# Moving one sum and its gate activation in the first and the last of eight output pairs

## The chip, the cores and the metric

The kernel runs on one core of a Trainium2 chip. The metric is the device time of one execution in microseconds (us). Times of before: a median of 366.15 us over three runs, from 365.76 to 366.25.

The engines are named as the profile names them: PE is TensorE (matmuls; PEld its weight loads), DVE is VectorE, ACT is ScalarE, POOL is GpSimd, SP is the engine that issues most of the transfers (DMA).

## The reference, cut to what matters

```python
x = A_x                                    # (1, 2048, 512)
xn = layernorm(x)
s = irfft2(rfft2(xn) * (w_r + 1j * w_i))   # spectral branch, the "way back" ends it
h = layernorm(xn)
u = gelu(einsum("bsd,sf->bdf", h, w1) + b1)        # token MLP, hidden size 1792
y = einsum("bdf,fs->bds", u, w2) + b2
out = x + s * silu(y.transpose(0, 2, 1))           # the gate is silu(y)
```

## The kernel before

All matmuls are fp32 in effect: each operand is split into a high part (a rounded copy, made by ACT) and a low part (the rest, a subtraction on DVE), and three matmuls are accumulated: high by high, high by low, low by high.

The first 200 us or so compute the layer norms, the first transform, the hidden layer (`u`) and the filter of the spectral branch. The last 160 us are the output stage, and the change lies there.

**Pairs.** The output has 16 row blocks of 128 tokens. They are handled as 8 pairs p = 0 to 7: block p (gate tile `g0`) and block p+8 (gate tile `g1`), each of 512 channels in two halves (`left_`, `right_`). A pair's product with the second weight matrix is a 2 by 2 block product, done in Strassen's manner with seven products instead of eight. A product (`products(p, n)`) is 21 matmuls of 256 columns. Its number n names the form of `u` that it reads: 1 is `fd`, 2 and 3 are `fa`, 5 and 6 are `fc`, 4 and 7 are `fb` in the profile. The products run in the order `ORDER = (1, 2, 5, 6, 3, 7, 4)`, into three PSUM areas: `bx` (one of two banks, by pair), `by`, `bz`.

**Sums of a pair.** Copies of partial products (`p1`, `p5`, `v2`, on ACT) and sums on DVE (all named `c` in the profile) give the four results:

- after product 2: `c11 = by + p1`, the left half of `g0` (its gate activation is issued after product 6);
- after product 3: `c12 = bz + v2`, the right half of `g0`. This is the sum that the change moves. In the profile it is `c<-ps,v`;
- after product 7: `c22 = bx + p5`, the right half of `g1` (`c<-ps,p`, as `c11` is);
- product 4 goes on accumulating in `bx`, the bank that `c22` reads, so its first matmul waits for `c22`. The left half of `g1` is gated straight from that bank.

A gate activation is one Silu on ACT, `g<-c,b2t` in the profile.

**Weights of the products.** `w2_forms()` is a generator of weight tiles `w2f`, each made by one ACT copy of 128x896 (high part) and one DVE subtraction (low part), from tiles `a12`, `a11`, `a21` (profile: `a`) and `s1`, `s4` (profile: `s`), which are loaded by SP and, for the sums of blocks, added to by POOL. There are three `w2f` buffers. The loop takes the next weights by `next(wforms)` after each product, about three products ahead: after product 3 of pair 0 come the weights of product 1 of pair 1, called `1_1` here, made from the `a12` tile that is loaded for pair 1.

**The way back of the spectral branch.** For each pair: `yt` copies (ACT and DVE), small matmuls (`even_channels`, `odd_channels`: `ps<-cd,yt`), then sums on DVE (`unfolded`: the tiles `es`, then two operations that write `y`), then eight matmuls (`spectral`: `ps<-y,cft`), and then `finish`, which multiplies by the gate and writes the block out. `SLOTS` lists by hand behind which product each piece stands. In pairs 0 to 6 the spectral matmuls and the multiplications run one pair late. In the last pair they follow at once: the `es` sums stand behind product 6, the two `y` operations behind product 3, the spectral matmuls behind product 7 and in front of product 4.

**Order.** In this stage every engine's instructions keep the program's order (`Kept`), so a position in the loop is a position in the queue of DVE, ACT, PE and SP.

In the loop, `k` counts the positions in `ORDER`; product 3 is `k == 4`. `more` is false in the last pair only.

Of the kernel before, what the change touches and what calls it, by code (L numbers as in the profile page):

```python
# [141 lines left out]
def spectral_mixer_kernel(tc, x, w1, b1, w2, b2, wk, we, wx, c_f, c_ft, c_d, c_i, c_g, c_h, out):  # L142
# [7 lines left out]
    def mirrored(t, turned):  # L150
        v = t.rearrange("p (h q c) -> p h q c", q=2, c=P)
        return v[:, :, 0], v[:, :, 1, ::-1] if turned else v[:, :, 1]
# [9 lines left out]
    with tc.tile_pool(name="ps", bufs=1, space=PSUM) as psp, ExitStack() as left, ExitStack() as right:  # L162
# [345 lines left out]
        for j in range(NJ):  # L508
            more = j + 1 < NJ
# [275 lines left out]
        for n in range(8):  # L785
            a, b, c, d, e, f = PACE[n]
# [51 lines left out]
        def sums_of_blocks():  # L838
            added_up("a12", "s1")
            added_up("a11", "a12")  # L840
# [58 lines left out]
        left_, right_, whole = slice(0, HD), slice(HD, D), slice(0, D)  # L899
        quarter_rows = slice(0, P), slice(P, HD)  # L900

        def banks(p):
            return ps[:, 2 + p % 2, :HD], ps[:, 4, :HD], ps[:, 5, :HD]

        def products(p, n):

            wf = ready.pop(0)
            bx, by, bz = banks(p)
            o = {1: bx, 6: bx, 7: bx, 4: bx, 2: by, 5: bz, 3: bz}[n]

            for a, (wi, ui) in enumerate(((0, 0), (0, 1), (1, 0))):
                for m, i in enumerate(FORMS):
                    T.matmul(o, wf[:, wi, i], form_parts(n, i)[ui], start=m + a == 0 and n in (1, 2, 5),
                             stop=m == NH - 1 and a == 2, skip_group_check=n in (6, 3, 7, 4))

        def copied(name, src, where):
            t = where.tile([P, HD], F32, name=name, tag=name.split("_")[0], bufs=1)
            step(A.activation(t, src, AF.Copy))
            return t
# [25 lines left out]
        def new_gates(p):  # L945
            return [fp.tile([P, D], F32, name=f"g{j}", tag="g", bufs=4) for j in (p, p + NP)]
# [6 lines left out]
        def gathered(p):  # L953


            yt = fp.tile([P, 2, 4, 2, 64], F32, name=f"yt{p}", tag="yt")
            yts[p] = yt
            for i, j in enumerate((p, p + NP)):
                for h in range(2):
                    to = yt[:, i, :, h ^ i].rearrange("p b (s c) -> p b s c", c=2)  # L960
                    yield V.tensor_copy(to, ey[:, :, h::2, j]) if i else A.activation(to, ey[:, :, h::2, j], AF.Copy)
# [4 lines left out]
        def even_channels(p):  # L966


            for i in range(2):
                for s in range(2):  # L970
                    at = slice(128 * i + 64 * s, 128 * i + 64 * s + 64)
                    for e in range(2):
                        for r, rows in enumerate((slice(0, 64), slice(64, P))):
                            T.matmul(ps[64 * e:64 * e + 64, 6 + r, at], yts[p][rows, i, 2 * s, e], ci[rows, 2 * s, :64],
                                     start=True, stop=True)
# [8 lines left out]
        def unfolded(p):  # L984

            es, y = new_sums(p) if p else first_sums
            e0, e1 = (es[:, :, k].rearrange("p i b c -> p i (b c)") for k in range(2))
            first, odd = ps[:, 6, :256].rearrange("p (i s c) -> p i s c", s=2, c=64), ps[:, 6:8, 256:]
            other = y.rearrange("p i h q c -> p (i h q c)")[:, :257]
            A.activation(other, ps[:, 7, :257], AF.Copy)  # L990
            other = other[:, :256].rearrange("p (i s c) -> p i s c", s=2, c=64)

            V.tensor_add(es[:, :, 1, :, :64], first, other)
            V.tensor_sub(es[:, :, 1, 0, :63:-1], first[:, :, 0], other[:, :, 0])
            V.tensor_sub(es[:, :, 1, 1, :63:-1], other[:, :, 1], first[:, :, 1])
            V.tensor_add(e0, e1, odd)
            V.tensor_sub(e1, e1, odd)
            yield
            u, v = es[:, :, :, 0], es[:, :, :, 1]
            V.tensor_add(y[:, :, :, 0], u, v)  # L1000
            yield
            V.tensor_sub(y[:, :, ::-1, 1], u, v)
            ys[p] = y.rearrange("p i h q c -> p i (h q c)")
            yield
# [9 lines left out]
        def gate(g, j, cols, src, scale):  # L1014
            A.activation(g[:, cols], src, AF.Silu, bias=b2t[:, j:j + 1], scale=scale)

        def summed(name, a, b):
            t = fp.tile([P, HD], F32, name=name, tag="c", bufs=2)
            V.tensor_add(t, a, b)
            return t  # L1020

        def finish(g, j, cols):
            r = last_rows[:, j // NP] if last_rows is not None else fp.tile([P, D], F32, name=f"r{j}", tag="r", bufs=2)
            for to, a, b in zip(mirrored(r[:, cols], True), mirrored(ps[:, j // NP, cols], False), mirrored(g[:, cols], False)):
                V.tensor_mul(to, a, b)
            if last_rows is not None:
                for part in quarter_rows if cols is left_ else (cols,):
                    V.tensor_add(r[:, part], r[:, part], xr[j // NP][:, part])
            for queue, (rows, tokens) in zip((SY, SY if cols is right_ else A), halved):
                if last_rows is None:  # L1030
                    G.dma_start(out[tokens, j, cols], r[rows, cols], accum_op=ALU.add)
                else:
                    queue.dma_start(out[tokens, j, cols], r[rows, cols])
# [4 lines left out]
        for p in range(NP):  # L1038
            j0, j1 = p, p + NP
            more = p + 1 < NP  # L1040
            if p:
                gates[p] = new_gates(p)
            g0, g1 = gates[p]
            bx, by, bz = banks(p)
            slot, plan = SLOTS[min(p, 2) + (not more)]
            gathering = gathered(p)
            for k, n in enumerate(ORDER):
                started = not p and k < 2
                if not started:
                    products(p, n)  # L1050
                if n == 1 and p:
                    p1 = copied(f"p1_{p}", bx, w2p)
                elif n == 5:
                    p5 = copied(f"p5_{p}", bz, fp)
                elif n == 6:
                    v2 = copied(f"v2_{p}", bx, fp)
                elif n == 7:
                    c22 = summed(f"c22_{p}", bx, p5)
                if not started:
                    ready.extend(w for w in [next(wforms, None)] if w is not None)  # L1060
                if n == 2:
                    c11 = summed(f"c11_{p}", by, p1)
                elif n == 6:
                    gate(g0, j0, left_, c11, 1.0)
                elif n == 3:
                    gate(g0, j0, right_, summed(f"c12_{p}", bz, v2), 1.0)
                elif n == 7:
                    gate(g1, j1, right_, c22, -1.0)
                elif n == 4:
                    for cols in (left_,) if more else quarter_rows:  # L1070
                        gate(g1, j1, cols, bx[:, cols], -1.0)
                if not p and k == slot - 1:
                    even_channels(p)
                if k == slot:
                    for part in PARTS[p]:
                        {"S": spectral, "E": even_channels, "O": odd_channels}[part](p - (part == "S"))
                    yts.pop(p)
                    pieces = unfolded(p)
                    if p:
                        for g, j in zip(gates.pop(p - 1), (j0 - 1, j1 - 1)):  # L1080
                            finish(g, j, whole)
                for what in plan.get(k, ""):
                    next(gathering if what == "g" else pieces)
                if more and n == 7:
                    sums_of_blocks()
                if not more and k == 2:
                    xr = [where.tile([P, NH * P], F32, name=f"xr{i}", tag="s1", bufs=1)[:, :D] for i, where in enumerate((w2p, fp))]
                    for to, j in zip(xr, (j0, j1)):
                        for rows, tokens in halved:
                            SY.dma_start(to[rows], x[tokens, j])  # L1090
                if not more and k == 5:
                    spectral(p)
                    last_rows = fp.tile([P, 2, D], F32, name="rows", tag="yt")
                    finish(g0, j0, whole)
                    finish(g1, j1, right_)
# [38 lines left out]
```

## Time and profile before

| | |
|---|---|
| median of 3 runs | 366.15 us (365.76 to 366.25) |
| the profiled execution, its own time | 366.07 us |
| its span in the trace | 364.3 us |
| PE busy | 357.4 us, 98% |
| DVE busy | 306.4 us, 84% |
| ACT busy | 211.1 us, 58% |
| POOL busy | 87.2 us, 24% |
| the chain that ended last, by engine | PE 90%, DVE 3%, DMA 3%, ACT 2%, issue 1% |

The span is the stretch that the trace covers; the execution's own time is 1.77 us longer. The chain that ended last is followed back from the last instruction, at each step to what released it. The rows stand in a section below.

### The profile page before, as it was taken

What the parts mean: (1) busy time and instruction counts of PE and PEld (TensorE: products, weight loads), DVE (VectorE), ACT (ScalarE), POOL (GpSimd) and SP (SyncE); (2) the same over time, 40 slices, a digit from 0 to 9 for tenths busy, and PEclk for the clock granted to TensorE, in tenths of its full rate; (3) what the DMA queues carried; (4) which work ended last, traced back from release to release, by engine and by line L of the source; (5) the groups of instructions that cost most, each with busy time, mean ns of one, the idle gap of its engine ahead of it and who ended that gap; (6) DMA issues with size and microseconds to landing.
All of it is one profiled execution on the core that took longest, in us unless ns stands there. A gap on an engine that the chain in (4) does not pass through costs nothing.

```text
span 364.3 us, 8851 instructions
## 1 busy us (share of the span) xinstructions
PE 357.4 (98%) x3476; PEld 310.0 (85%) x3476; DVE 306.4 (84%) x590; ACT 211.1 (58%) x385; POOL 87.2 (24%) x134
## 2 busy tenths in 40 slices
PE   8999999999999999999999999999999999999994
PEld 7788888888777778777888999989898989898993
DVE  4899999967699996999995988687787869696984
ACT  4887788867534426755237875656464545565541
POOL 4233333323222012220120001050403122140330
PEclk9999999999999999999999999999999999999999
DMA  6987899406695697996567298688888989898624
GB/s 207 236 201 197 210 275 305 183 0 161 163 269 191 189 248 183 253 243 186 185 238 154 101 230 176 165 189 201 195 186 212 180 222 158 222 168 228 113 30 87
DMA packets 33294, 68.66 MB, mean 188 GB/s; under 512 B 4613, under 2 KB 19381, under 8 KB 33125
## 3 DMA queue, kind: packets, MB, share of 16 engines
q1 hardware_dynamic: 24276, 42.44, 42.3%
q0 software_dynamic: 8496, 25.01, 32.0%
q10 hardware_dynamic: 480, 0.66, 0.6%
q8 instruction: 27, 0.44, 0.5%
q14 instruction: 15, 0.11, 0.1%
HBM read 59.70 MB, written 8.13 MB: 186 GB/s over the span
## 4 chain that ended last, share of the span: by engine, by line
PE 90%; DVE 3%; DMA 3%; ACT 2%; issue 1%; ACTq 0%; DVEq 0%; SPq 0%
PE ps L139 90%; DMA a<-in_w_dram 2%; DMA w1r<-in_w_dram 1%; DVE es L139 1%; DVE a L836 1%; ACT w2f L139 1%; DVE r L139 0%; ACT fc L363 0%; DVE y L139 0%; DVE c L139 0%; DVE w2f L824 0%; ACT w2f L820 0%; DVE rows L139 0%; ACT u L355 0%; DVE fc L368 0%
## 5 line engine op out<-in xcount | busy, mean ns | idle before, releaser
L139 PE MATMUL ps<-h,w1h 128*128 128x512 f32 x400 | 116.3, 397 | 0.0
L139 PEld LDWEIGHTS ps<-h,w1h 128*128 128x128 f32 x400 | 72.9, 188 | 19.8 <-issue 4.9
L139 PE MATMUL ps<-h,w1l 128*128 128x512 f32 x200 | 67.6, 390 | 0.0
L139 DVE TENSOR_TENSOR w2f<-a,w2f 128x896 fp32r<-128x896 f32 x36 | 39.2, 1090 | 22.1 <-ACT w2f L139 22.1
L139 ACT ACTIVATE w2f<-a 128x896 fp32r<-128x896 f32 x36 | 36.8, 1022 | 13.3 <-PE ps L139 6.7
L139 PEld LDWEIGHTS ps<-h,w1l 128*128 128x128 f32 x200 | 37.5, 188 | 8.1
L139 PE MATMUL ps<-fb,w2f 128*128 128x256 f32 x336 | 41.9, 279 | 0.6 <-DVE c L139 0.6
L139 POOL DMA_DIRECT2D s<-in_w_dram x14 | 18.4, 1312 | 95.8 <-DMA s<-in_w_dram 59.5
L139 PE MATMUL ps<-fa,w2f 128*128 128x256 f32 x336 | 41.2, 277 | 0.0
L139 PEld LDWEIGHTS ps<-fb,w2f 128*128 128x128 f32 x336 | 39.7, 188 | 1.5 <-DVE c L139 1.5
L139 PE MATMUL ps<-fc,w2f 128*128 128x256 f32 x336 | 39.8, 277 | 0.0
L139 PEld LDWEIGHTS ps<-fa,w2f 128*128 128x128 f32 x336 | 39.7, 188 | 0.0
L139 PEld LDWEIGHTS ps<-fc,w2f 128*128 128x128 f32 x336 | 39.0, 188 | 0.0
L155 ACT ACTIVATE w1h<-w1s 128x512 fp32r<-128x512 f32 x26 | 16.2, 631 | 25.0 <-PE ps L139 10.9
L139 POOL DMA_DIRECT2D out_dram<-r x28 | 23.6, 1278 | 28.5 <-DVE r L139 28.5
L667 POOL DMA_DIRECT2D xc<-xc x16 | 9.8, 619 | 69.9 <-ACT xc L665 54.7
L308 POOL TENSOR_TENSOR ey<-t 128x256 f32<-128x256 f32 x16 | 15.7, 979 | 43.8 <-DVE t L306 43.8
L139 ACT ACTIVATE w2f<-s 128x896 fp32r<-128x896 f32 x15 | 15.4, 1023 | 13.6 <-PE ps L139 12.3
L469 DVE TENSOR_TENSOR w1l<-w1r,w1h 128x384 fp32r<-128x384 f32 x32 | 21.3, 670 | 0.0
L139 ACT ACTIVATE g<-c,b2t 128x256 f32<-128x256 f32 x24 | 12.1, 505 | 15.0 <-DVE c L139 15.0
L139 PE MATMUL ps<-fd,w2f 128*128 128x256 f32 x168 | 20.6, 277 | 0.0
L268 ACT ACTIVATE h<-x,nbm,rsm 128x256 f32<-128x256 f32 (+1 forms) x34 | 18.4, 592 | 3.5 <-DVE nbm L263 2.9
(132 smaller groups left out, 606.4 us busy)
## 6 DMA issues: line engine op xcount, KB each, us to landing
a<-in_w_dram SPq DMA_DIRECT2D x22, 448.0 KB, 4.2
wt<-in_wk_dram POOLq DMA_DIRECT2D x16, 512.0 KB, 6.0
s<-in_w_dram SPq DMA_DIRECT2D x16, 448.0 KB, 4.2
s<-in_w_dram POOLq DMA_DIRECT2D x16, 448.0 KB, 6.7
w1s<-in_w_dram SPq DMA_DIRECT2D x52, 128.0 KB, 5.0
w1r<-in_w_dram SPq DMA_DIRECT2D x28, 192.0 KB, 5.5
xc<-xc POOLq DMA_DIRECT2D x16, 256.0 KB, 3.0
out_dram<-in_x_dram SPq DMA_DIRECT2D x4, 960.0 KB, 6.9
```

The costliest lines, as they stand in the source:

```text
L139: return lambda *args, **kw: self.keep(operation(*args, **kw))
L155: return A.activation(hi, src, AF.Copy), V.tensor_sub(lo, src, hi.bitcast(F32))
L268: keep(A.activation(to, v, AF.Identity, bias=m["nb"][:, i], scale=m["rs"][:, i, 1:2]))
L308: G.tensor_add(ey[:, 0::3, :, j], a, b)
L469: keep(V.tensor_sub(dst, src, hi.bitcast(F32)))
L667: keep(G.dma_start(*(v.rearrange("p s t c -> p s (t c)") for v in (there[c::2], here[1 - c::2, ::-1]))))
L836: step(V.tensor_add(cur[name], cur[name], cur[other]))
```

## The change

The sum `c12` and its gate activation become one helper, `right_gate`, which is called at one of three places behind product 3:

- in pair 0, in front of `next(wforms)`: `c12` on DVE and its gate on ACT come ahead of the making of weights `1_1` (the high part on ACT, the low part on DVE). Before, they came behind it;
- in pairs 1 to 6, where the sum stood before;
- in pair 7, behind the pieces of the plan: `c12` comes after the two `y` operations. Before, it came ahead of them. In pair 7 no weights are left to be made at that place.

No instruction is added or removed.

```diff
+        def right_gate(p, g, bz, v2):
+            gate(g, p, right_, summed(f"c12_{p}", bz, v2), 1.0)
...
                 elif n == 7:
                     c22 = summed(f"c22_{p}", bx, p5)
+                elif n == 3 and not p:
+                    right_gate(p, g0, bz, v2)
                 if not started:
                     ready.extend(w for w in [next(wforms, None)] if w is not None)
...
-                elif n == 3:
-                    gate(g0, j0, right_, summed(f"c12_{p}", bz, v2), 1.0)
+                elif n == 3 and p and more:
+                    right_gate(p, g0, bz, v2)
...
                 for what in plan.get(k, ""):
                     next(gathering if what == "g" else pieces)
+                if n == 3 and not more:
+                    right_gate(p, g0, bz, v2)
```

## Rows read from the trace of the kernel before

**Rows 1.** The page, busy time and share of the span by engine.
```profile
PE 357.4 (98%) x3476; PEld 310.0 (85%) x3476; DVE 306.4 (84%) x590; ACT 211.1 (58%) x385; POOL 87.2 (24%) x134
```

**Rows 2.** Chain that ended last, by time: start us, us, what.
```profile
210.57 5.51 DMA a<-in_w_dram
...
218.25 0.76 DVE c L139 x2
...
219.05 129.17 PE ps L139 x1283
...
354.25 0.33 DVE c L139
354.59 1.21 DVE y L139 x2
...
355.93 3.78 PE ps L139 x29
```

**Rows 3.** Timeline, pair 0: start us, us, engine line op, [idle before <-releaser].
```profile
212.77 2.64 PE L139 MATMUL ps<-fa,w2f 128*128 128x256 f32 x21
...
215.25 2.63 PE L139 MATMUL ps<-fb,w2f 128*128 128x256 f32 x21
215.59 0.54 DVE L139 COPY yt<-ey 128x256 f32<-128x256 f32 x2
...
216.19 1.02 ACT L139 ACTIVATE w2f<-a 128x896 fp32r<-128x896 f32 x1 [0.84 <-DMA a<-in_w_dram]
217.24 1.09 DVE L139 TENSOR_TENSOR w2f<-a,w2f 128x896 fp32r<-128x896 f32 x1 [1.11 <-ACT w2f L139]
...
217.81 0.69 PE L139 MATMUL ps<-cd,yt 64*64 64x64 f32 x32
218.25 0.42 DVE L139 TENSOR_TENSOR c<-ps,v 128x256 f32<-128x256 f32 x1
218.58 0.42 DVE L139 TENSOR_TENSOR c<-ps,p 128x256 f32<-128x256 f32 x1
218.70 0.51 ACT L139 ACTIVATE g<-c,b2t 128x256 f32<-128x256 f32 x1 [1.49 <-DVE c L139]
...
219.05 2.74 PE L139 MATMUL ps<-fb,w2f 128*128 128x256 f32 x21 [0.55 <-DVE c L139]
219.12 1.01 ACT L139 ACTIVATE w2f<-a 128x896 fp32r<-128x896 f32 x1
```

**Rows 4.** Instructions of tile yt, 212 to 220 us: ns min/median/max, first and last start.
```profile
L139 DVE COPY yt<-ey x2: 314/314/315, 215.6 to 215.8; 128x256 f32<-128x256 f32 x2
```

**Rows 5.** The page's DMA issues: count, KB each, median us to landing.
```profile
a<-in_w_dram SPq DMA_DIRECT2D x22, 448.0 KB, 4.2
```

**Rows 6.** Timeline, pair 7.
```profile
353.10 2.63 PE L139 MATMUL ps<-fb,w2f 128*128 128x256 f32 x21
354.17 0.42 DVE L139 TENSOR_TENSOR c<-ps,v 128x256 f32<-128x256 f32 x1
354.50 1.28 DVE L139 TENSOR_TENSOR y<-es 128x512 f32<-128x512 f32 x2
...
355.77 0.42 DVE L139 TENSOR_TENSOR c<-ps,p 128x256 f32<-128x256 f32 x1
...
355.93 1.09 PE L139 MATMUL ps<-y,cft 64*64 64x512 f32 x8 [0.20 <-DVE y L139]
356.23 0.51 ACT L139 ACTIVATE g<-c,b2t 128x256 f32<-128x256 f32 x1 [1.09 <-DVE c L139]
...
357.15 0.76 DVE L139 TENSOR_TENSOR rows<-ps,g 128x256 f32<-128x256 f32 x2 [0.96 <-PE ps L139]
```

**Rows 7.** Windows: busy time of each engine, granted clock of PE, DMA share, GB/s.
```profile
218.20:219.05 0.85, 0.30 (x22) 0.16 (x12) 0.80 (x3) 0.35 (x1) 0.00 (x0) 1.00 0.95 384
...
219.00:348.00 129.00, 128.95 (x1283) 123.31 (x1283) 104.12 (x165) 71.25 (x115) 31.90 (x37) 1.00 0.84 183
```

## The prediction

> **What bounds the kernel.** I read the page's busy times first: PE is busy for 98% of the span, DVE for 84%, ACT for 58% [rows 1]. Then the chain that ended last, in order of time: from 219.05 us it is one unbroken run of 1283 matmuls on PE for 129.17 us [rows 2], and in that window PE is busy for 128.95 of 129.00 us [rows 7]. So in the output stage a delay of PE is a delay of the end, nothing later gives it back, and only what shortens or lengthens a hole in PE's work counts. There are two such holes, and both lie at the two places that the change touches. The timeline shows them close up.
>
> First hole, pair 0 [rows 3]. PE ends the 32 small matmuls at 217.81 + 0.69 = 218.50 and starts product 4 at 219.05: 0.55 us, released by "DVE c". This is c22, which must have read the bank that product 4 writes. The chain behind it [rows 2, 3]: the a12 tile, issued at 210.57, lands 5.51 us later (216.08); ACT makes the high part of weights 1_1 (start 216.19); DVE the low part (217.24); then c12 (218.25), then c22 (218.58), then PE (219.05). c22 waits for neither weight nor c12; it only stands behind them on DVE.
>
> Second hole, pair 7 [rows 6]. Product 7 ends at 353.10 + 2.63 = 355.73, the spectral matmuls start at 355.93, and 0.20 us of this is a wait for "DVE y". On DVE, c12 (354.17) stands ahead of the two y operations (354.50 to 355.78), and the chain that ended last runs through both [rows 2].
>
> **Pairs 1 to 6.** The call stands where the sum stood, so no queue changes. Cost nothing, and no cover is needed.
>
> **Pair 0: the sum leaves one queue position and the gate takes a worse one.** On DVE c12 goes from behind the low part of 1_1 to in front of it. c22 stays behind the low part. If the low part kept its time, c22 would come earlier by one c12: start to start 218.58 - 218.25 = 0.33 us. That is the saving.
>
> But c12's gate is moved too, and on ACT it now stands in front of the high part of 1_1. ACT is in order, as is DVE, so the high part waits for the gate, the gate for c12, and c12 for its place on DVE. Step by step:
>
> - c12's inputs are there: product 3 ends at 212.77 + 2.64 = 215.41 [rows 3]. DVE is not free: it makes two yt copies from 215.59 on, 0.54 us for both, each 0.314 [rows 3, 4]. So the second starts at 215.59 + 0.54 - 0.31 = 215.82, and the step between two of them is 0.23. c12 starts at 215.82 + 0.23 = 216.05 and ends 0.42 later, at 216.47.
> - The gate starts 0.03 after c12's end (218.25 + 0.42 = 218.67, gate at 218.70): 216.50.
> - The high part starts 0.42 behind the gate's start (218.70 to 219.12, where the next high part follows that gate): 216.92. Before, 216.19, when a12 had just landed.
> - The low part starts 1.05 behind the high part's start (216.19 to 217.24): 217.97.
> - c22 starts 1.01 behind the low part's start (217.24 to 218.25, where c12 followed): 218.98.
> - Product 4 starts 0.47 behind c22's start (218.58 to 219.05): 219.45.
>
> So product 4 starts **0.40 us later**: +0.73 for the high part held back, -0.33 for c12. Queued behind the waiting gate on ACT are the high parts of 1_1 and of the next weights; who waits for 1_1's low part in time is only c22, and behind it PE. The weights themselves have room: product 1 of pair 1 comes after product 4. SP and POOL have no transfer among the moved instructions; the transfers that follow wait for weight parts made after product 4 and shift with PE.
>
> Bounds of this term. Write h for the time at which ACT could start the high part by the transfer. Before, PE starts at h + 2.86 (219.05 - 216.19); after, at the later of h and 216.92, plus 2.53. If a12 lands so late that h is past 216.92, the gate is hidden and the term is -0.33. The two are equal at h = 216.59, a landing 0.40 us later than here. At the other end, 1_1 reuses the weight buffer of product 3 (three buffers, and it is made three tiles after that product's), so h is at least 215.41; then the old c22 would be held only by product 7's end (215.25 + 2.63 = 217.88), the old hole would be gone, PE would start at about 218.50, and the term is 219.45 - 218.50 = +0.95. The landing of 5.51 us is already longer than the median of 4.2 us over 22 such transfers [rows 5], so an earlier one is somewhat more at hand than a later one. I take the profiled landing: +0.40.
>
> **Pair 7: the sum leaves the path.** The y operations start where c12 stood, 354.50 - 354.17 = 0.33 us earlier, and end at 355.45; with the 0.15 us that PE took to start after y's end (355.78 to 355.93), the spectral matmuls could start at 355.60. PE gets there only when product 7 is through. By its modelled end, 355.73, the gain is the 0.20 us that the row calls idle. But where PE follows on without a wait it starts ahead of the modelled end: small matmuls at 217.81 after an end of 217.88 [rows 3], 0.07 us. So 355.73 - 0.07 = 355.66, and the gain is 355.93 - 355.66 = **0.27 us**; bounds 0.20 and 0.33.
>
> The Trainium skill bears on this choice (Perfetto Trace Analysis, "Tensor Engine Instruction (MATMUL, LD_WEIGHTS)"): a matmul's end in the trace is computed from its size and not observed. The trace agrees as far as starts ahead of ends show it. By the idle figure alone, taken at its word, the gain would be 0.20 and the net sum 0.20; by the starts it is what I take.
>
> c12 now starts at about 355.37 and is done by 355.79; its gate then takes ACT to about 356.33. c22 at 355.77 still waits for product 7, as before [rows 6], so its gate at 356.23 moves by at most 0.1. The multiplications that need both gates wait for the spectral matmuls' end and start at 357.15, then at 356.88, 0.1 us or more after the second gate's end (356.23 + 0.51 = 356.74). So c12 costs nothing in its new place; without that cover, were the y operations 0.5 us later, the gates would hold the multiplications.
>
> **Sum.** +0.40 - 0.27 = +0.13 us. The profiled execution took 366.07 us (span 364.3 and 1.77 around it), 0.08 below the median of 366.15: forecast 366.20 for it, 366.28 for a median. A measurement of this kernel can tell about 0.2% (0.73 us) from no change, so the forecast is no measurable change.
>
> **Rivals.**
>
> 1. *The transfer hides the gate.* If a12 lands 0.8 us or more later than in the profiled execution, both places gain: -0.33 - 0.27 = -0.60, 365.55 us. For it: DMA share is 0.95 in the window at the hole [rows 7], so the landing can slip. Against it: 5.51 us is already long [rows 5]. This is also the most that the change can bring, since c22 stays behind the low part.
> 2. *The transfer is early as a rule.* Then the old kernel has no hole in most executions and the gate makes one: +0.95 - 0.27 = +0.68, 366.83 us. For it: the median landing [rows 5]. Against it: the profiled execution shows the hole and is no slower than the median.
> 3. *The wait in pair 0 costs nothing*, since ACT's two instructions come in another order than I read from the code, and c22 moves by 0.1 us or less: only pair 7 counts, -0.27, 365.88 us. Against it: in the rows DVE and ACT follow the program's order.
> 4. *The longer hole slows PE's clock* (the other side, beyond what can be told from no change). The hole grows to 218.50 to 219.45. At half clock a product of 21 matmuls would take about twice its 2.6 us: +2.6 us for one, about 368.9 us. It decides once the granted clock falls after that hole. Against it: with PE busy for 0.30 of 0.85 us it stayed at 1.00 [rows 7].
>
> **Chances.** The forecast (both mechanisms as sized, 366.0 to 366.6) 0.60. Rival 1 0.13, rival 2 0.14, rival 3 0.08, rival 4 0.02, and 0.03 for what I don't see. Rivals 1 and 2 stop just short of 0.73 us; with a spread between runs of 0.49 us some of each crosses it: 0.04 of the first makes "faster", 0.05 of the second "slower". With the rest split (0.02 to faster, 0.01 and the clock's 0.02 to slower): faster 0.06, same 0.86, slower 0.08. The range reaches from rival 1 less 0.15 to rival 2 plus 0.15: 365.4 to 367.0.
>
> **What would show it.** Right: in pair 0 the order on ACT is g, then w2f of 1_1 at about 216.9, and PE's idle time at "DVE c" is about 0.95 instead of 0.55; in pair 7 "DVE y" no longer releases PE and the spectral matmuls follow product 7 directly; the granted clock is 1.00. Wrong: the hole in pair 0 shrinks (a12 landed later than 216.8, or the order differs), or a new hole appears after 219 us, as at weights made later than their product.

## The result, and the profile after

| | median | lowest to highest | runs |
|---|---|---|---|
| before | 365.95 us | 365.31 to 367.37 | 18 |
| after | 366.69 us | 366.07 to 367.32 | 18 |

The ratio is 1.0015, 95% interval 1.0008 to 1.0022: about 0.55 us slower (0.3 to 0.8 by the interval), as the means have it (366.58 against 366.03). The medians are further apart, 0.74 us. The median of after lies inside the forecast range (365.4 to 367.0). By the ratio the change is under the 0.2% (0.73 us) that the prediction called no measurable change, by the medians it is right at it; the forecast size was 0.13 us. The profiled execution of after took 366.79 us (span 365.0).

The single times of after fall into two groups, 5 from 366.07 to 366.30 us and 13 from 366.65 to 367.32 us (12 of them up to 366.79). This will matter more than the change itself.

Pair 0 in the timeline of after (start us, us, engine line op, idle before; compare [rows 3]):

```profile
215.58 0.53 DVE L139 COPY yt<-ey 128x256 f32<-128x256 f32 x2
...
216.04 0.41 DVE L139 TENSOR_TENSOR c<-ps,v 128x256 f32<-128x256 f32 x1
...
216.48 0.51 ACT L139 ACTIVATE g<-c,b2t 128x256 f32<-128x256 f32 x1 [1.16 <-DVE c L139]
216.90 2.10 ACT L139 ACTIVATE w2f<-a 128x896 fp32r<-128x896 f32 x2
...
217.92 1.09 DVE L139 TENSOR_TENSOR w2f<-a,w2f 128x896 fp32r<-128x896 f32 x1 [1.47 <-ACT w2f L139]
218.92 0.42 DVE L139 TENSOR_TENSOR c<-ps,p 128x256 f32<-128x256 f32 x1
...
219.40 2.74 PE L139 MATMUL ps<-fb,w2f 128*128 128x256 f32 x21 [0.92 <-DVE c L139]
```

ACT waits 1.16 us for c12, the gate goes first, and the high part of 1_1 starts at 216.90 instead of 216.19. The hole of PE in front of product 4 is 0.92 us instead of 0.55. In the chain that ended last the transfer of a12 is gone, and the gate is in its place (compare [rows 2]; start us, us, what):

```profile
216.04 0.42 DVE c L139
...
216.48 0.04 ACT g L139
...
216.90 0.99 ACT w2f L139
...
218.92 0.43 DVE c L139
...
219.40 141.00 PE ps L139 x1402
```

From 219.40 to 360.40 the chain is PE alone; the way through y in pair 7, which stood in the chain of before, is no longer in it. Pair 7 (compare [rows 6]):

```profile
353.83 1.41 DVE L139 TENSOR_TENSOR es<-es,ps 128x512 f32<-128x512 f32 x2
...
354.08 2.63 PE L139 MATMUL ps<-fb,w2f 128*128 128x256 f32 x21
355.27 1.29 DVE L139 TENSOR_TENSOR y<-es 128x512 f32<-128x512 f32 x2
356.48 0.42 DVE L139 TENSOR_TENSOR c<-ps,v 128x256 f32<-128x256 f32 x1
...
356.71 1.09 PE L139 MATMUL ps<-y,cft 64*64 64x512 f32 x8
...
357.93 0.76 DVE L139 TENSOR_TENSOR rows<-ps,g 128x256 f32<-128x256 f32 x2 [0.70 <-ACT g L139]
```

From the start of product 7 to the spectral matmuls it is 356.71 - 354.08 = 2.63 us; before, 355.93 - 353.10 = 2.83. The idle time of PE in front of them is gone. The first rows start 1.22 us behind the spectral matmuls' start, as before (357.15 - 355.93), but now a gate is named as their last releaser.

So the two mechanisms give 0.35 us (219.40 against 219.05) and -0.20 us. But PE had lost another 0.65 us by the time it came to pair 7, in a stretch without any wait. The PE timelines of both kernels show where. Before, product 4 of pair 1 and then products 1, 2, 5 and 6 of pair 2:

```profile
239.86 2.63 PE L139 MATMUL ps<-fb,w2f 128*128 128x256 f32 x21
242.32 2.54 PE L139 MATMUL ps<-fd,w2f 128*128 128x256 f32 x21
244.71 2.54 PE L139 MATMUL ps<-fa,w2f 128*128 128x256 f32 x21
247.09 4.92 PE L139 MATMUL ps<-fc,w2f 128*128 128x256 f32 x42
```

After, the same products:

```profile
240.20 2.72 PE L139 MATMUL ps<-fb,w2f 128*128 128x256 f32 x21
242.76 2.63 PE L139 MATMUL ps<-fd,w2f 128*128 128x256 f32 x21
245.23 2.63 PE L139 MATMUL ps<-fa,w2f 128*128 128x256 f32 x21
247.70 5.11 PE L139 MATMUL ps<-fc,w2f 128*128 128x256 f32 x42
```

A product takes 2.38 us from start to start before (244.71 to 247.09) and 2.47 us after (245.23 to 247.70), with the same 21 matmuls and no idle time. Call these the fast and the slow cadence: 113 and 118 ns for a matmul. Before, pair 1 runs slowly and pairs 2 to 6 fast; after, pairs 1 and 2 run slowly. One pair at the slow cadence costs 7 times 0.09, some 0.6 us, which is also the distance between the two groups of times. (That the groups of after come from this is not shown: its one profile is from the upper group.)

### The profile page after: what moved, and what is told of

Same layout as the page of the kernel before. It is cut to its first block, busy times and chain, and to the rows that moved or that the text cites. A ratio compares the mean times of both kernels' runs of the same rounds, so it can differ in the third digit from the quotient of the medians.

```text
span 365.0 us, 8851 instructions
## 1 busy us (share of the span) xinstructions
PE 358.3 (98%) x3476; PEld 310.9 (85%) x3476; DVE 306.9 (84%) x590; ACT 211.0 (58%) x385; POOL 87.2 (24%) x134
## 4 chain that ended last, share of the span: by engine, by line
PE 91%; DVE 3%; ACT 2%; issue 1%; DMA 1%; ACTq 1%; DVEq 0%
PE ps L139 91%; DMA w1r<-in_w_dram 1%; DVE a L836 1%; ACTq L452 1%; DVE w2f L139 1%; ACT w2f L820 1%; DVE c L139 0%; ACT fc L363 0%; DVE w2f L824 0%; ACT h L268 0%; ACT w2f L139 0%; DVE rows L139 0%; DVE h L469 0%; ACT u L355 0%; DVE fc L368 0%
```

## The experiments

"Slow pairs" counts, among pairs 1 to 6, those whose products run at 2.47 us in the profiled execution. Product 4 is left out: it stands behind the pair's small matmuls, and in pairs 1 to 6 its run goes on into the products of the next pair. Pairs 0 and 1 are slow in all 14 profiles, pairs 3 to 6 in g2 and g3 alone. Before was timed anew with each group of kernels, with medians of 365.89 to 366.05 us. Times "from the stage's first product" are counted from the first product of the output stage, which starts at 202.60 to 203.37 us (202.88 in before, 202.85 in after): so much the first 200 us differ from execution to execution.

| kernel | median us | runs | ratio to before, 95% interval | profiled us | slow pairs |
|---|---|---|---|---|---|
| before | | | | 366.07 | 1 |
| after | 366.69 | 18 | 1.0015 [1.0008, 1.0022] | 366.79 | 2 |
| e1, pair 0's part only | 366.83 | 8 | 1.0024 [1.0014, 1.0035] | 366.34 | 1 |
| e2, pair 7's part only | 365.78 | 11 | 0.9995 [0.9986, 1.0004] | 366.04 | 2 |
| e3, sum without its gate | 365.89 | 11 | 1.0002 [0.9994, 1.0011] | 366.35 | 2 |
| e4, c22 before weights | 365.54 | 11 | 0.9989 [0.9980, 0.9997] | 365.55 | 2 |
| f1, odd channels into the hole | 368.72 | 9 | 1.0066 [1.0045, 1.0087] | 366.43 | 2 |
| f2, one small matmul more | 367.24 | 5 | 1.0039 [1.0027, 1.0051] | 367.31 | 2 |
| f3, two more | 366.84 | 7 | 1.0043 [1.0029, 1.0058] | 366.47 | 1 |
| f4, e4 and f1 together | 365.78 | 11 | 0.9999 [0.9991, 1.0008] | 365.78 | 2 |
| g1, f4 with odd channels first | 365.05 | 11 | 0.9969 [0.9959, 0.9980] | 365.03 | 1 |
| g2 and g3, f1 again | | 1 each | | 368.76, 368.77 | 6, 6 |
| g4, e1 again | | 1 | | 366.24 | 1 |

### e1 and e2: one part at a time

```diff
 # e1, against after
-                elif n == 3 and p and more:
+                elif n == 3 and p:
...
-                if n == 3 and not more:
-                    right_gate(p, g0, bz, v2)
 # e2, against after
-                elif n == 3 and not p:
-                    right_gate(p, g0, bz, v2)
...
-                elif n == 3 and p and more:
+                elif n == 3 and more:
```

e1: 

> Only pair 0's part of the change; pair 7 as before. Theory A (the gate in front of the high part, plus a cadence of the matmuls that is drawn anew): high part of 1_1 at about 0.7 us behind the transfer's landing of before, hole in front of product 4 of pair 0 about 0.92 us instead of 0.55, product 4 starts 0.35 us later; behind it whole pairs of products run either at 2.38 or at 2.47 us for 21 matmuls, so the end moves by 0.35 us plus 0 or 0.6 us, and the single times fall in two groups some 0.6 us apart. Rival B (the moved weights shift transfers and DVE work so that PE runs slower in pair 2, always): pair 2 is at 2.47 us in every profile in which pair 0's sum is moved, and the times form one group, 0.95 us above before.

e2: 

> Only pair 7's part; pair 0 as before. Theory A: the wait for y in front of the spectral matmuls is gone, 0.2 to 0.3 us less from product 7 of pair 7 on; hole in pair 0 as before, about 0.55 us; median 0.2 us under before (0.05%), less than single times scatter. Pair 2 may run at either cadence. Rival B: pair 2 always at 2.38 us as in the profile of before. Rival C (pair 7's part brings nothing, since the new c12 in front of c22 or the gates hold the end): same time as before and the first multiplication of the last rows waits for a gate.

e1 has after's hole of 0.92 us, and its pair 7 still waits 0.20 us for y. Its times lie at 366.26 to 366.48 (3) and 366.81 to 367.15 us (5). In its profile pair 2 is fast, so B falls: the moved sum does not force the slow cadence. e2 keeps before's order in pair 0 and yet shows pairs 1 and 2 slow, which B excluded too. From product 7 of pair 7 to the spectral matmuls e2 needs 2.62 us, as after does:

```profile
353.25 2.63 PE L139 MATMUL ps<-fb,w2f 128*128 128x256 f32 x21
...
355.87 1.09 PE L139 MATMUL ps<-y,cft 64*64 64x512 f32 x8
```

Its first rows are released by a gate in the profile (0.70 us "ACT g", as in after), as C said, so the gates' cover is used up. But they start 1.22 us behind the start of the spectral matmuls (357.09 against 355.87), as before (357.15 against 355.93, [rows 6]): C's "same time" is not borne out by the trace. The times (ratio 0.05% under before) cannot tell.

### e3: the sum in front, its gate behind

```diff
 # against before, in pair 0 only
+                elif n == 3 and not p:
+                    c12 = summed(f"c12_{p}", bz, v2)
...  next(wforms) here
+                elif n == 3 and not p:
+                    gate(g0, j0, right_, c12, 1.0)
```

> In pair 0 the sum c12 stands in front of the weights 1_1 and its gate stays behind their high part; pair 7 as before. Theory A: the loss in pair 0 comes from the gate alone, so the high part starts at the landing of a12 again, c22 comes 0.33 us earlier than before, the hole falls from 0.55 to about 0.22 us. Rival D (the loss comes from c12 being waited for on DVE, gate or not): the hole stays at 0.9 us. The end also moves by multiples of 0.6 us with the cadence.

```profile
216.17 1.02 ACT L139 ACTIVATE w2f<-a 128x896 fp32r<-128x896 f32 x1 [1.01 <-DMA a<-in_w_dram]
...
218.23 0.42 DVE L139 TENSOR_TENSOR c<-ps,p 128x256 f32<-128x256 f32 x1
...
218.71 2.74 PE L139 MATMUL ps<-fb,w2f 128*128 128x256 f32 x21 [0.40 <-DVE c L139]
```

The high part starts at the landing again, and c22 follows 2.06 us behind it, against 2.39 before (218.58 - 216.19): 0.33 us saved, as theory A had it. The hole is 0.40 and not 0.22 us, because the transfer landed later in this execution: the high part stands 216.17 - 202.69 = 13.48 us behind the stage's first product, and 13.31 before (216.19 - 202.88). D falls. The whole kernel is no faster by its median. Why is not shown: the profile has two slow pairs, but it is one of two executions at 366.35 and 366.38 us, and of the nine others (365.80 to 365.96) none was profiled.

### e4: c22 in front of the weights

```diff
-                if not started:
+                for _ in range(0 if started or (not p and n == 3) else 2 if not p and n == 7 else 1):
                     ready.extend(w for w in [next(wforms, None)] if w is not None)
```

> As after, and in pair 0 the weights 1_1 are made behind c22, so that neither the transfer nor the gate stands in front of it. Theory A: c22 starts when product 7 ends, product 4 follows the small matmuls at once, the hole is under 0.1 us; 0.9 us less than after and 0.75 us less than before at equal cadence; product 1 of pair 1 finds its weights ready. Rival E (the weights 1_1 are then late for product 1 of pair 1, or later ones for theirs): a new wait of PE behind product 4 of pair 0, and no gain over before.

```profile
217.53 0.69 PE L139 MATMUL ps<-cd,yt 64*64 64x64 f32 x32
217.71 0.42 DVE L139 TENSOR_TENSOR c<-ps,p 128x256 f32<-128x256 f32 x1 [1.53 <-ACT w2f L139]
218.05 2.08 DVE L139 TENSOR_TENSOR w2f<-a,w2f 128x896 fp32r<-128x896 f32 x2
218.19 2.65 PE L139 MATMUL ps<-fb,w2f 128*128 128x256 f32 x21
```

c22 starts as soon as product 7 is through, product 4 follows the small matmuls without idle time, and no later wait of PE appears, so E falls. From the stage's first product, product 4 starts at 15.59 us, against 16.17 in before and 16.54 in after. The kernel is 0.1% faster than before, less than the hole alone would give. In the profiled execution a second slow pair took back about as much as the hole had been worth; that holds for this execution, as the times (365.03 to 366.02) scatter by more than a pair's 0.6 us.

### f1 and f4: work into the hole

```diff
                 if not p and k == slot - 1:
                     even_channels(p)
+                    odd_channels(p)
                 if k == slot:
-                    for part in PARTS[p]:
+                    for part in PARTS[p] if p else ():
```

f1 is this on after, f4 is this on e4.

f1: 

> As after, but in pair 0 the eight odd-channel matmuls (1.05 us, from 221.97 in the trace of after) are issued ahead of product 4, into the hole. Theory A: the hole of 0.92 us is filled by work that was to be done anyway, product 4 still starts at about 219.4, product 1 of pair 1 follows it at once and starts about 0.8 us earlier than in after (16.5 + 2.5 = 19.1 us behind the stage's first product instead of 19.9); the end moves by -0.8 us and multiples of 0.6 us with the cadence. Rival (the weights 1_1 or the buffers then bind): a new wait of PE at product 1 of pair 1 and less than half of that gain.

f4: 

> As after, with c22 in front of the weights 1_1 in pair 0 and the odd-channel matmuls ahead of product 4. Theory A: the hole was already gone with the first of the two, so the second only takes away one change between small matmuls and products (a first step of some 0.2 us instead of 0.12): within 0.1 us of the kernel with c22 in front, at equal cadence. If the cadence is set at the entry into a run of products, pair 1 enters straight from product 4 and keeps the cadence of product 4.

In f1's profile product 1 of pair 1 stands 19.12 us behind the stage's first product (19.93 in after, 222.78 - 202.85): the 0.8 us were gained, and no wait came for them. Yet seven of nine executions took 368.68 to 369.15 us, 2 us more than after. f4 took 365.78 us in a narrow group, 0.24 us more than e4. In the profiles, which have the same slow pairs, f4 needs 36.36 us from the stage's first product to product 4 of pair 1 and e4 36.30, within the 0.1 us expected; another 0.14 us lie in the first 200 us.

### f2 and f3: a small matmul repeated

```diff
 # against after; 1 in f2, 2 in f3
+                    for _ in range(1 if p == 1 else 0):
+                        T.matmul(ps[64:P, 7, 192:256], yts[p][64:P, 1, 2, 1], ci[64:P, 2, :64], start=True, stop=True)
                     yts.pop(p)
```

f2: 

> As after, with one of pair 1's small matmuls repeated once in front of its product 4 (about 0.02 us more work for PE, same result written twice). Theory L (the cadence of a run of products, 2.38 or 2.47 us for 21 matmuls, is set by how PE enters it): the share of executions in the upper group of times (13 of 18 in after, 0.6 us above the lower) changes, or the pairs that run slowly in the profile do; the groups stay some 0.6 us apart. Rival M (the cadence is set by what other engines and transfers do beside PE): the same share and the same slow pairs as in after, all times 0.02 us later.

f3: 

> As the one before it, with the small matmul repeated twice (about 0.03 us more). Theory L: once more another share or other slow pairs; with groups 0.6 us apart. Rival M: as after.

f2's five times lie in one group, 367.06 to 367.31 us; f3's in two, 366.47 to 366.84 (4) and 367.85 to 368.25 us (3). The repetition (two matmuls in the trace for each `T.matmul`) cost more than I expected: from the stage's first product, product 4 of pair 1 starts 0.43 us later than in after with one and 0.55 us with two. But f3, with more work, was 0.84 us shorter than f2 in the profiled executions (0.19 of it from the first 200 us), and had one slow pair where f2 had two. That alone doesn't decide between L and M, since after itself falls into two groups: five executions of f2 in the upper one can be chance (13 of 18 to the fifth power is 0.2). Against M speaks f3's upper group, 1.0 to 1.8 us above its lower one, which after does not show; no profile was taken from it. Nor were the others' positions left alone: PE's delay of 0.43 or 0.55 us moves its matmuls against their work.

### g1: the other order in the hole

```diff
 # against f4
-                    even_channels(p)
-                    odd_channels(p)
+                    odd_channels(p)
+                    even_channels(p)
```

> As the kernel with both edits in pair 0 (c22 in front of the weights, odd-channel matmuls ahead of product 4), but the odd-channel matmuls come first and the even-channel ones second, so that PE enters product 4 from another kind of matmul. Theory L: no wait of PE in pair 0 or 7, the same work, and yet the time can differ by multiples of 0.6 us, in steps of whole pairs at 2.38 or 2.47 us for a product; if product 4 of pair 0 is entered at 2.38 us, pair 1 is too, and the kernel is at 365.1 us. Rival M: the same time as with the other order, 365.8 us.

365.05 us, 0.73 under f4 with the same work, and no execution of one lies among those of the other (364.83 to 365.27 against 365.68 to 366.00). The profiles differ in pair 2, slow in f4 (2.48 us from product to product) and fast in g1 (2.38):

```profile
241.65 2.63 PE L139 MATMUL ps<-fd,w2f 128*128 128x256 f32 x21
244.13 2.63 PE L139 MATMUL ps<-fa,w2f 128*128 128x256 f32 x21
```

```profile
241.47 2.54 PE L139 MATMUL ps<-fd,w2f 128*128 128x256 f32 x21
243.85 2.54 PE L139 MATMUL ps<-fa,w2f 128*128 128x256 f32 x21
```

So M's forecast of the same time falls. Product 4 of pair 0 and pair 1 are slow in both: the edit did not change the cadence at the entry that it touches, but at the next one, in front of which the two kernels are alike (product 4 of pair 1 starts at 36.36 and 36.35 us from the stage's first product). That the time is the 365.1 us expected is luck, as the expectation had it from pair 1. Of before's profiled execution it saves 1.04 us: 0.97 of this is 0.54 by the hole (19.02 instead of 19.56 us from the stage's first product to product 1 of pair 1), 0.20 in pair 7 (6.21 instead of 6.41 us from product 3 to product 4) and 0.23 in the first 200 us (202.65 instead of 202.88), with one slow pair in each. It is the fastest kernel of the study.

### g2, g3, g4: the same kernels again, for the other group

g2: 

> The kernel with the odd-channel matmuls moved into the hole, once more, for a profile from its upper group of times (7 of 9 executions lay between 368.68 and 369.15 us, the profiled one at 366.43 us). Theory L: in such an execution about four more pairs run at 2.47 us for a product than in the profile already taken (2.3 to 2.7 us by 0.6 us), and no new wait of PE is seen. Rival (another cause of 2.4 us): a wait, or a change in the first 200 us, with the same cadence of the pairs.

g3: 

> The same kernel a third time, with the same expectation: whichever group its time falls into, the number of pairs at 2.47 us for a product accounts for the difference from the other profiles of it, at 0.6 us each.

g4: 

> The kernel with only pair 0's part of the change, once more. Its profiled execution at 366.34 us had pair 2 at 2.38 us for a product; five of its eight executions were 0.5 us or more longer. Theory L: an execution near 366.85 us shows pair 2 at 2.47 us, one near 366.3 us at 2.38 us, with the same hole of 0.92 us in pair 0 either way. Rival: the two groups differ in the hole or in the first 200 us.

g2 and g3 fell into f1's upper group, and all six pairs are slow, four more than in f1's own profile; so are the first five products of pair 7. From the stage's first product to the end of the span f1 needs 161.2 us, g2 164.3 and g3 164.3: the cadence costs 3.0 to 3.1 us. The times differ by 2.3 us only, because f1's stage began 0.7 us later (203.37 against 202.65 and 202.69). So the sum in the expectation, four pairs at 0.6 us, comes close by luck: it lacks pair 7, and the first 200 us did change. The rival's cause of the longer time falls, as no wait appears and the first 200 us differ the other way. Windows of the same 92 us, g2 (busy time and instructions by engine, granted clock, DMA share, GB/s):

```profile
258.00:350.00 92.00, 92.00 (x889) 88.16 (x886) 73.53 (x118) 49.21 (x80) 24.05 (x28) 1.00 0.83 176
```

and f1:

```profile
258.00:350.00 92.00, 92.00 (x935) 86.77 (x929) 74.93 (x121) 51.11 (x83) 24.17 (x29) 1.00 0.84 179
```

PE is busy throughout in both, at a granted clock of 1.00 and nearly the same DMA share, and gets through 889 matmuls in one and 935 in the other. Only the step differs: in g2 a product takes 281.43 to 283.90, 2.47 us; in f1 281.43 to 283.81, 2.38 us:

```profile
281.43 2.63 PE L139 MATMUL ps<-fd,w2f 128*128 128x256 f32 x21
283.90 2.64 PE L139 MATMUL ps<-fa,w2f 128*128 128x256 f32 x21
```

```profile
281.43 2.54 PE L139 MATMUL ps<-fd,w2f 128*128 128x256 f32 x21
283.81 2.54 PE L139 MATMUL ps<-fa,w2f 128*128 128x256 f32 x21
```

g4 fell into e1's lower group, with pair 2 fast and the hole of 0.92 us, as expected for that group; the upper group of e1 was not caught in a profile.

## Why the prediction was right, and where it fell short

**Pair 0: +0.40 forecast, +0.37 measured.** The steps came out one by one: c12 216.05 forecast and 216.04 in the trace, gate 216.50 and 216.48, high part 216.92 and 216.90, low part 217.97 and 217.92, c22 218.98 and 218.92, product 4 219.45 and 219.40. (From the stage's first product it is 16.54 instead of 16.17 us, hence 0.37; by the clock of the trace 0.35, as the stage began 0.03 us earlier.) That the gate and not the sum costs is shown by e3. The forecast that the transfer leaves the path is borne out too: in the eight profiles of after, e1, f1, f2, f3, g2, g3 and g4 product 4 starts 16.54 or 16.55 us behind the stage's first product, while in before, e2 and e3, which wait for the transfer, it is 16.17, 15.97 and 16.02. So the loss depends on the landing of before: against e2's execution it would be 0.57. The upper bound of the term, +0.95, was sized rightly too: e4, whose c22 waits for product 7 and not for the transfer, starts product 4 0.96 us ahead of after.

**Pair 7: -0.27 forecast, -0.20 measured.** The term was mis-sized at the step "the y operations start where c12 stood". Before, the es operations ended at 352.84 + 1.41 = 354.25:

```profile
352.84 1.41 DVE L139 TENSOR_TENSOR es<-es,ps 128x512 f32<-128x512 f32 x2
```

c12 does not read what they had just written, and it started 0.08 us ahead of their end, at 354.17 (0.08 in e1 too). y reads them: in after es ends at 353.83 + 1.41 = 355.24, and y starts 0.03 behind, at 355.27 (0.03 in e2 too). So y ends at 356.56 and PE starts 0.15 us later, at 356.71, the step that it took from y in before. The prediction chose between the idle figure of 0.20 and a gain with a starting lead of 0.07. The Trainium skill (Perfetto Trace Analysis, "Tensor Engine Instruction (MATMUL, LD_WEIGHTS)") says that such an end is computed and not observed, and the prediction went by the starts. The result agrees with the idle figure, but it does not decide that question, since product 7's modelled end (354.08 + 2.63 = 356.71) and the step from y give the same moment. That c12 costs nothing in its new place is borne out, but only just: the second gate ends 357.84, 0.09 us ahead of the rows.

**The sum.** The two terms as measured give +0.17 us. The lower group of after, 366.07 to 366.30 us, lies 0.0 to 0.2 us above the profiled execution of before. What the prediction did not have is the cadence. The step that doesn't hold is its first conclusion, "only what shortens or lengthens a hole in PE's work counts". It named a new hole or a clock as what could go wrong behind 219 us, and it was neither: the granted clock stayed at 1.00, no wait appeared, and PE still lost a pair's 0.65 us. The profiled executions add up with it: +0.37 in pair 0, +0.65 by pair 2's cadence, -0.20 in pair 7, -0.09 because pair 7's product 4 ran at the fast cadence in after, and -0.03 in the first 200 us are 0.70 of the 0.72 us between them (366.79 and 366.07). Rivals 1, 3 and 4 are refuted: product 4 of pair 0 came later and not earlier, the hole grew by 0.37 us, and the clock held. Of rival 2 the landing's scatter is real (0.57 against e2), but no profile showed the old hole gone: it is 0.34 us in e2. The median of after, 366.69, lies nearer to rival 2's 366.83 than to the forecast's 366.28, and by the time alone one would have taken that rival; the trace, with +0.37 and not +0.95 in pair 0, refutes it. "No measurable change" held, at 0.55 us against 0.73, but in part by luck: more than half of the 0.55 us has a cause that was not forecast, and the medians are 0.74 us apart. f1, with a hole filled, is 0.66% slower than before.

**What is shown of the cadence, and what stays open.** Shown: it differs at equal kernel, clock and work (f1 against g2 and g3), it makes f1's two groups of times, and an edit of nothing but the order of PE's matmuls shifts it (g1 against f4). That it makes the groups of after, e1 and f3 as well fits their distances, but of each only one group was profiled. Read over all 14 profiles: inside a run of products it never changed. In every run at the fast cadence a matmul starts 110 ns (median) behind the start of its own weight load, in every run at the slow one 115 ns, and in the stretches that I compared closely (239 to 241 us in before and after) the next weight load starts 2 to 4 ns behind the matmul in both. At the small matmuls ahead of product 4 in pairs 1 to 6, 2.38 us was followed by 2.38 in 53 of 53 cases, 2.47 by 2.47 in 19 and by 2.38 in 12. At pair 7's block of small matmuls, which stands in another order, 2.38 became 2.47 in 12 of 12 cases and 2.47 became 2.38 in the other 2. Open: what decides. The sequence of matmuls in the entry does not do it alone. At product 4 of pair 2 f1 goes over to the fast cadence and g2 doesn't, with the same program: the last six steps of PE in front agree to 1 ns, and the starts on ACT and DVE in the 6 us before to 12 ns; the first difference in PE's steps is the second step of the run, 113 ns in f1 and 120 in g2. No run here tells what lies behind it. Therefore it is also open whether the share of the upper group in after, 13 of 18, belongs to the change or to where its hole happens to end.

## What to carry to other kernels

Move a sum without its consumer where the consumer sits on another in-order engine: here the sum alone saved 0.33 us and its gate, carried along, cost 0.7. Ask what the waiting instruction needs that its neighbours do not: c22 needed no weights, and putting it first removed the hole altogether. And where a kernel is bound by PE, look at the start-to-start time of equal groups of matmuls, and at the single times for groups, before a difference of some tenths of a per cent is put down to an edit.

## What the hardware showed that I had not expected

- Two steady cadences of the same run of matmuls with one weight load each, 128x256: 2.38 and 2.47 us for 21, at a granted clock of 1.00, without waits, kept from entry to end of a run; 0.65 us for a pair, and 3.0 to 3.1 us in the output stage between executions of one kernel (f1 against g2 and g3). The difference lies between the start of a weight load and that of its matmul: 110 and 115 ns.
- One more `T.matmul` of 64 rows and 64 columns (two matmuls in the trace) behind eight matmuls of 128 by 128 moved the next product by 0.43 us, while 32 small matmuls in a row take 0.69 us.
